# A new order for the first stage of an attention and two-FFN kernel on one core

## Chip, cores and metric

The kernel runs on one core of one Trainium2 chip. The metric is the device time of one execution in microseconds (us): the median of 3 runs before the change is 557.69 us (557.67 to 558.53).

## What is computed

A chunked attention with decays (a state-space form), then an FFN with a squared ReLU, then a bilinear FFN. Cut to what matters here:

```python
# x: 4 x 8 x 768 x 32, a: 4 x 8 x 768, B, C: 4 x 8 x 768 x 16; chunk by chunk along the 768
cum = np.cumsum(log(clip(a)), axis=-1)
L = np.exp(cum[:, :, :, None] - cum[:, :, None, :]) * causal
y_intra = einsum('bhij,bhjd->bhid', einsum('bhin,bhjn->bhij', C, B) * L, x)
y_inter = einsum('bhin,bhnd->bhid', C, state) * exp(cum)[..., None]
state = exp(sum(la))[..., None, None] * state + einsum('bhjn,bhjd->bhnd', B * decay_from_j, x)
# then, on 3072 tokens of 256:
x = relu(x @ w_in) ** 2 @ w_out          # 256 -> 2048 -> 256
x = ((x @ w1) * (x @ w2)) @ w3 @ w_out2  # 256 -> 1024 -> 1024 -> 256
```

## The kernel before

**Tiles.** The 3072 tokens are cut into six tiles of 512. For each tile the attention is worked out in chunks of 96 tokens; two chunks make a unit. The first stage, `startup`, does the six chunks (units 0, 1, 2) of tile 0, prepares units 3 and 4, and converts the first pieces of the weights. After it a loop goes through phases: A (the squared-ReLU FFN) and B (the bilinear FFN) of each tile, with the attention of the next tile placed between the matmuls. Weights arrive as 64-bit numbers, 512 KB a piece (`conv_load`), and are made into a high and a low float part by ScalarE (`conv_words`: L196, L198; `conv_parts`: L230), VectorE (`conv_bits`: L207, L210; `split_lo`, L141) and partly GpSimd (L228).

**The chain of the first stage.** `a` and `masks` are loaded; the logarithm (L343), then matmuls with the masks (L419, L455) give `e_first` (L422) and `dec` (L459). For a unit and each quarter q of its heads `unit_e1` (L663, L668 on TensorE, L671 on ScalarE) gives the decay factors e. `unit_pad` (L602) and `unit_bi` (L607) lay out C and B, `unit_g0` (L637) multiplies them into four PSUM banks, and `unit_m0` (L679, VectorE) multiplies a bank with its e. `chunk_pre` (L578, GpSimd) scales the chunk's x and B, `state` (L717 on TensorE, L724 on ScalarE) hands the state to the next chunk, and `value` (L755, then L144 and L141) gives the output of a chunk in `xt`. The first matmul of phase A (L819) needs all of `xt`.

**Order.** `startup` runs under `in_order()`, so each engine carries out its instructions in the order in which the function's calls stand. All loads go through SyncE's queue by `dma` (L93), in program order; a load also waits until the load eight places earlier has landed. B and C of the first batch come in two parts: the first 256 columns (`batch_load(s, 0, 1)`) and the rest (`batch_load(s, 1, 3)`); s is 0 for B, 1 for C. `unit_split` writes the split B and C of a later unit to DRAM (`hl_d`), and `unit_bc` loads them back in twelve small loads as `bt` and `cb`, for the matmuls of L618.

Of the kernel before, what the change touches and what calls it, by code (L numbers as in the profile page):

```python
# [7 lines left out]
F32 = mybir.dt.float32  # L8
# [7 lines left out]
P = 128  # L16
# [42 lines left out]
def kernel(  # L59
# [19 lines left out]
    nc = tc.nc  # L79
# [9 lines left out]
    ps_g = ctx.enter_context(tc.tile_pool(name="ps_g", bufs=2, space=PSUM))  # L89
    ps_y = ctx.enter_context(tc.tile_pool(name="ps_y", bufs=1, space=PSUM))  # L90

    def dma(out, in_):
        tc.keep_in_program_order(nc.sync.dma_start(out=out, in_=in_))  # L93

    keep = tc.keep_in_program_order

# [34 lines left out]
    def new_tmp():  # L131
        return tmp.tile([P, 512], F32, tag="tmp", name="tmp")
# [148 lines left out]
    pick = [gp.tile([P, H, P], F32R, tag="gp", name="pick") for k in range(2)]  # L281
    ident = wts.tile([P, P], F32R, tag="wa9", name="ident")
    nmask = act1.tile([P, P], F32R, tag="cmask", name="nmask")[:, :CH]
    m_rel = new_tmp()
    m_oth = new_tmp()
    la = new_tmp()[:, :256]
    lps = new_tmp()
    lp = lps[:, :192].rearrange("p (k c) -> p k c", k=3)
    lp4 = lps[:, 192:320].rearrange("p (v d c) -> p v d c", v=4, d=2)

    def constants():
        def diagonal(v, base=0, step=1, fill=1.0):
# [12 lines left out]
        raw = wts.tile([P, 512], F32, tag="wa10", name="raw")
        sel, one, low = raw[:, :64].rearrange("r (p c) -> r p c", p=4), raw[:, 64:192], raw[:, 192:192 + CH]
        nc.gpsimd.memset(cb.bitcast(F32), 0.0)
        nc.gpsimd.memset(raw[:, :192 + CH], 0.0)
        for base in (0, -16):
            diagonal(sel, base, 32, -1.0)  # L310
        diagonal(one.unsqueeze(1), 0, 0)
        causal(low.unsqueeze(1), NEVER)
        nc.gpsimd.memset(id2, 0.0)
        for p in range(4):
            diagonal(id2[32 * p:32 * p + 32].unsqueeze(1), 0, 0)
        nc.gpsimd.memset(idc, 0.0)
# [15 lines left out]
    def decays_load(k):
        if k == 0:
            dma(out=la, in_=a)
        elif k == 1:
            dma(out=m_rel, in_=masks[:, 0:512])
        else:
            c = (slice(256, 392), slice(0, 256))[k - 2]
            dma(out=m_oth[:, c], in_=masks[:, 512 + c.start:512 + c.stop])

    def decays_ln():
        nc.vector.tensor_scalar(out=la, in0=la, scalar1=1e-6, scalar2=1.0, op0=ALU.max, op1=ALU.min)
        nc.scalar.activation(  # L343
            lp.rearrange("p k (u h) -> p u k h", u=8), la[:, :192].rearrange("p (u k h) -> p u k h", u=8, k=3), AF.Ln
        )

        def put(copy, v, r, r_in, k):
            copy(lp4[r, v], lp[r_in, k, :2 * H].unsqueeze(1).to_broadcast([r.stop - r.start, 2, 2 * H]))

        put(nc.scalar.copy, 0, slice(0, P), slice(0, P), 0)  # L350
        put(nc.scalar.copy, 3, slice(0, P), slice(0, P), 2)
# [3 lines left out]
        warm = const.tile([P, 1], F32, name="warm")  # L355
        nc.scalar.activation(warm, la[:, :1], AF.Exp)

    def rel(b, i, n, nb=1):
# [120 lines left out]

    batch_0 = {}  # L480

    def batch_load(s, u0, u1):
        if s not in batch_0:
            batch_0[s] = wts.tile([P, S], F32, tag=f"wa{15 - s}", name="raw0")
        dma(
            out=batch_0[s].rearrange("p (u t) -> p u t", t=UT)[:, u0:u1],
            in_=raw_in[u0:u1].rearrange("u p (s t) -> s p u t", s=2)[s],
        )
# [117 lines left out]
    def unit_bi(c0, c1):  # L606
        nc.vector.tensor_copy(bi[:, c0:c1, :CH], batch_0[0][:, c0 * CH:c1 * CH].rearrange("p (c i) -> p c i", i=CH))  # L607
# [445 lines left out]
    def startup():  # L1053
        ys = {}

        def y0(g):
            ys[g] = new_mm()[:, :2 * CH].rearrange("p (h i) -> p h i", h=2)
            chunk_y_mm(g, ys[g])

        ds = [y_bank[:, 256 * (g % 2):256 * (g % 2) + 256] for g in range(FIRST[1])]  # L1060

        def state(g):
            chunk_ds(g, ds[g])
            if g + 1 < FIRST[1]:
# [10 lines left out]
        decays_load(0)  # L1075
        decays_load(1)
        decays_load(2)
        decays_load(3)
        batch_load(0, 0, 1)
        batch_load(1, 0, 1)  # L1080
        chunk_xb(0)
        chunk_xb(1)
        batch_load(0, 1, 3)
        batch_load(1, 1, 3)
        chunk_xb(2)
        chunk_xb(3, "w124")
        chunk_xb(4, "w125")
        chunk_xb(5, "w126")
        conv_load(1)
        unit_load(4)  # L1090
        conv_load(2)
        picks, rounded = constants()
        decays_ln()
        picks(0, nc.vector)
        rounded()
# [3 lines left out]
        decays_e_first()  # L1099
        picks(1, nc.gpsimd)  # L1100
        nc.vector.tensor_copy(bi[:, :, CH:], id2.unsqueeze(1).to_broadcast([P, FIRST[1], 32]))
        decays_cols()
        unit_bi(0, 2)
        unit_pad(0)
        chunk_pre(0)
        for q in range(4):
            unit_e1(0, q)
        unit_g0(0)
        unit_bi(2, 6)
        unit_pad(1)  # L1110
        chunk_pre(1)
        state(0)
        m0(0)
        chunk_pre(2)
        unit_e1(1, 0)
        unit_e1(1, 1)
        unit_split(3, "w120")
        state(1)
        unit_rows(bt)
        chunk_pre(3)  # L1120
        value(0)
        unit_e1(1, 2)
        unit_e1(1, 3)
        unit_pad(2)
        unit_g0(1)
        state(2)
        chunk_pre(4)
        m0(1)
        value(1)
        conv_load(2)  # L1130
        unit_bc(3)
        chunk_xb(6)
        unit_e1(2, 0)
        unit_e1(2, 1)
        conv_words(0)
        state(3)
        chunk_pre(5)
        value(2)
        unit_e1(2, 2)
        unit_e1(2, 3)  # L1140
        conv_bits(0)
        unit_g0(2)
        state(4)
        value(3)
        decays_e(0)
# [6 lines left out]
        value(4)
        chunk_xb(7)
        conv_words(1)
        value(5)
        state(5)
        conv_load(1)
        conv_bits(1)
        unit_split(4, "w121")
        chunk_xb(8)  # L1160
        conv_load(1)
# [150 lines left out]
```

## Time and profile before

| | |
|---|---|
| median of 3 runs | 557.69 us |
| profiled execution, its own time | 559.61 us |
| its span from first to last instruction | 557.9 us |
| mean granted TensorE clock | 0.993 |
| TensorE matmul, busy | 544.0 us (98%) |
| VectorE, busy | 367.6 us (66%) |
| ScalarE, busy | 284.3 us (51%) |
| GpSimd, busy | 88.1 us (16%) |

Engines are named PE (TensorE), DVE (VectorE), ACT (ScalarE), POOL (GpSimd) and SP (SyncE). PE is busy for 98% of the span; of its 13.9 us of idle time some 10 lie before 100 us. A busy PE is not PE at its peak: the ends of its matmuls are modelled, and the granted clock says at which of its two levels (1.2 and 2.4 GHz) it ran.

### The profile page before, as it was taken

What the parts mean: (1) busy time and instruction counts of PE and PEld (TensorE: products, weight loads), DVE (VectorE), ACT (ScalarE), POOL (GpSimd) and SP (SyncE); (2) the same over time, 40 slices, a digit from 0 to 9 for tenths busy, and PEclk for the clock granted to TensorE, in tenths of its full rate; (3) what the DMA queues carried; (4) which work ended last, traced back from release to release, by engine and by line L of the source; (5) the groups of instructions that cost most, each with busy time, mean ns of one, the idle gap of its engine ahead of it and who ended that gap; (6) DMA issues with size and microseconds to landing.
All of it is one profiled execution on the core that took longest, in us unless ns stands there. A gap on an engine that the chain in (4) does not pass through costs nothing.

```text
span 557.9 us, 9140 instructions
## 1 busy us (share of the span) xinstructions
PE 544.0 (98%) x3340; PEld 448.5 (80%) x3340; DVE 367.6 (66%) x665; ACT 284.3 (51%) x543; POOL 88.1 (16%) x136
## 2 busy tenths in 40 slices
PE   7979999999999999999999999999999999999997
PEld 5757777889888888888888888888888888888886
DVE  5689999987989575576576556574566474554431
ACT  6699768877875322354333354342435332444332
POOL 7344750000000221004031004020012010000000
PEclk9889999999999999999999999999999999999999
DMA  8697592143454561067250066120173220100001
GB/s 235 231 307 225 176 374 91 39 152 114 164 173 126 135 160 53 0 156 177 68 133 17 16 156 170 24 79 1 36 168 100 57 70 0 39 0 2 0 1 38
DMA packets 56573, 59.46 MB, mean 107 GB/s; under 512 B 33360, under 2 KB 44624, under 8 KB 56528
## 3 DMA queue, kind: packets, MB, share of 16 engines
q1 hardware_dynamic: 56528, 58.88, 36.8%
q8 instruction: 26, 0.43, 0.3%
q14 instruction: 19, 0.16, 0.1%
HBM read 50.20 MB, written 8.65 MB: 105 GB/s over the span
## 4 chain that ended last, share of the span: by engine, by line
PE 81%; DVE 8%; ACT 4%; DMA 4%; issue 1%; SPq 1%; DVEq 0%; ACTq 0%
PE mm L819 43%; PE acc L866 19%; PE acc L919 10%; PE mm L257 4%; PE acc L928 2%; PE y L755 2%; PE g L618 2%; DVE gp L141 2%; DMA xb<-in_xb_dram 1%; DMA raw<-in_raw_dram 1%; DVE cvs L207 1%; DVE wa L141 1%; SPq L93 1%; DVE cvs L210 1%; DMA u<-in_w_dram 1%
## 5 line engine op out<-in xcount | busy, mean ns | idle before, releaser
L819 PE MATMUL mm<-xt,wa 128*128 128x512 f32 x576 | 148.7, 395 | 3.2 <-DVE wa L141 2.0
L849 ACT CAST gp<-tmp 128x512 fp32r<-128x512 f32 x144 | 89.3, 622 | 119.4 <-DVE tmp L907 64.3
L866 PE MATMUL acc<-gp,wa 128*128 128x512 f32 x576 | 146.4, 392 | 1.3 <-DVE gp L141 0.7
L141 DVE TENSOR_TENSOR gp<-tmp,gp 128x512 fp32r<-128x512 f32 x144 | 103.0, 718 | 62.7 <-ACT gp L849 61.9
L819 PE MATMUL mm<-x,w 128*128 128x512 f32 x576 | 143.4, 392 | 0.0
L819 PEld LDWEIGHTS mm<-xt,wa 128*128 128x128 f32 x576 | 107.4, 190 | 26.8 <-ACT tmp L833 2.4
L866 PEld LDWEIGHTS acc<-gp,wa 128*128 128x128 f32 x576 | 106.4, 188 | 24.5 <-DVE gp L141 1.5
L819 PEld LDWEIGHTS mm<-x,w 128*128 128x128 f32 x576 | 105.9, 188 | 21.7 <-ACT tmp L899 0.2
L833 ACT ACTIVATE tmp<-mm 128x512 f32<-128x512 f32 x96 | 57.3, 597 | 50.9 <-PE mm L819 50.2
L919 PE MATMUL acc<-gp,w3o 128*128 128x512 f32 x240 | 63.7, 391 | 0.0
L843 DVE TENSOR_TENSOR tmp<-tmp 128x512 f32<-128x512 f32 x68 | 46.9, 692 | 24.0 <-ACT tmp L833 23.5
L559 POOL TENSOR_SCALAR_AFFINE_SELECT e<-e 96x768 f32<-96x768 f32 x26 | 25.3, 985 | 236.3 <-DMA e<-e_d 228.9
L907 DVE TENSOR_TENSOR tmp<-tmp,mm 128x512 f32<-128x512 f32 x48 | 33.0, 687 | 42.9 <-PE mm L819 42.4
L919 PEld LDWEIGHTS acc<-gp,w3o 128*128 128x128 f32 x240 | 44.8, 188 | 9.4
L899 ACT COPY tmp<-mm 128x512 f32<-128x512 f32 x48 | 28.2, 587 | 41.0 <-PE mm L819 40.7
L578 POOL TENSOR_TENSOR xb<-xb,dec 96x256 f32<-96x256 f32 x32 | 23.1, 723 | 91.9 <-DMA xb<-in_xb_dram 89.2
L624 DVE TENSOR_TENSOR e<-g,e 128x384 f32<-128x384 f32 x52 | 27.6, 551 | 6.5 <-PE g L618 6.0
L257 PE MATMUL mm<-wo,w 128*128 128x256 f32 x128 | 23.7, 284 | 0.4 <-DVE w L141 0.3
L745 DVE SCALAR_TENSOR_TENSOR xb<-xb,through,y 32x64 f32<-32x64 f32 x72 | 20.3, 282 | 3.1 <-PE y L717 1.3
L257 PEld LDWEIGHTS mm<-wo,w 128*128 128x128 f32 x128 | 20.6, 190 | 2.0 <-DVE w L141 1.0
L618 PEld LDWEIGHTS g<-cb,bt 96*128 96x128 f32 x96 | 16.6, 190 | 3.3
L257 PE MATMUL mm<-wo2l,w 128*128 128x256 f32 x64 | 18.1, 283 | 0.0
(111 smaller groups left out, 476.9 us busy)
## 6 DMA issues: line engine op xcount, KB each, us to landing
u<-in_w_dram SPq DMA_DIRECT2D x24, 512.0 KB, 3.9
ua<-in_w_dram SPq DMA_DIRECT2D x16, 512.0 KB, 7.0
e<-e_d SPq DMA_DIRECT2D x40, 192.0 KB, 5.1
xb<-in_xb_dram SPq DMA_DIRECT2D x32, 192.0 KB, 3.8
bt<-hl_d SPq DMA_DIRECT2D x78, 48.0 KB, 2.1
hl_d<-gp SPq DMA_DIRECT2D x9, 384.0 KB, 2.6
cb<-hl_d SPq DMA_DIRECT2D x66, 48.0 KB, 2.0
out_dram<-gp SPq DMA_DIRECT2D x20, 128.0 KB, 3.0
```

Source lines behind the costliest of these rows:

```text
L141: return nc.vector.tensor_tensor(out=lo, in0=src, in1=hi.bitcast(F32), op=ALU.subtract)
L257: nc.tensor.matmul(acc[:, :DM], v[:, l, e % 4 * P:(e % 4 + 1) * P], wo2[1 + e // 2][r][:, e % 2 * DM:(e % 2 + 1) * DM], start=(n == 0), st ...
L618: nc.tensor.matmul(ps[:, 2 * pp:2 * pp + 2], w, un["c2"][:, pr, :, j * CH:(j + 1) * CH], start=True, stop=True)
L624: nc.vector.tensor_tensor(out=m, in0=ps, in1=m, op=ALU.mult)
L819: i = nc.tensor.matmul(ps, w[m][:, l, col + k * P:col + (k + 1) * P], rhs[k][:, r, :], start=((l, r, k) == (1, 0, 0)), stop=((l, r, k) == ...
L833: nc.scalar.activation(r, ps, AF.Relu)
L843: nc.vector.tensor_tensor(out=g32, in0=r, in1=r, op=ALU.mult)
L849: nc.scalar.copy(g[:, 0, :], d[k])
L866: i = nc.tensor.matmul(acc["x2", t][e], wa[m][:, l, 256 + e * P:256 + (e + 1) * P], g[:, r, :], start=(m == 0 and n == 0), stop=(m == MF - ...
L899: nc.scalar.copy(s, ps)
L907: nc.vector.tensor_tensor(out=p32, in0=prods[t, m], in1=ps, op=ALU.mult)
L919: nc.tensor.matmul(acc["o"][e].rearrange("p s e -> p (s e)"), w3o[m // 2][:, l, m % 2, e * P:(e + 1) * P], g[:, r, :], start=(m == 0 and n ...
```

## The change

Four things. The order of the calls in `startup` is another one. The products of `unit_m0` and the factors of `unit_e1` are called one quarter at a time and interleaved, where all four of a unit stood together. `masks` comes in one transfer of 904 columns into one tile, where it came in three into two tiles. The first parts of B and C are issued from ScalarE's queue, behind a small Ln that has its table loaded ahead of them. Besides, GpSimd's clearing of `cb` moves behind the making of the constants.

```diff
-    def dma(out, in_):
-        tc.keep_in_program_order(nc.sync.dma_start(out=out, in_=in_))
+    def dma(out, in_, eng=nc.sync):
+        tc.keep_in_program_order(eng.dma_start(out=out, in_=in_))
...
-    m_rel = new_tmp()
-    m_oth = new_tmp()
+    m_all = wts.tile([P, 904], F32, tag="wo0", name="masks")
+    m_rel, m_oth = m_all[:, :512], m_all[:, 512:]
...
         nc.vector.memset(lp4, 0.0)
+        nc.vector.memset(warm, 1.0)
+        nc.scalar.activation(warm, warm, AF.Ln)
...
-        nc.gpsimd.memset(cb.bitcast(F32), 0.0)
         nc.gpsimd.memset(raw[:, :192 + CH], 0.0)
...
         nc.gpsimd.memset(bt[64:96, :, :, CH:].bitcast(F32), 0.0)
+        nc.gpsimd.memset(cb.bitcast(F32), 0.0)
...
-    def batch_load(s, u0, u1):
+    def batch_load(s, u0, u1, eng=nc.sync):
...
+        picks, rounded = constants()
+        decays_load()
         chunk_xb(0)
         chunk_xb(1)
+        batch_load(0, 0, 1, nc.scalar)
+        picks(0, nc.vector)
+        batch_load(1, 0, 1, nc.scalar)
+        conv_load(1)
+        batch_load(1, 1, 3)
         batch_load(0, 1, 3)
...
+        unit_e1(0, 0)
...
+        unit_e1(1, 3)
         chunk_pre(0)
-        for q in range(4):
-            unit_e1(0, q)
+        unit_e1(0, 1)
+        unit_e1(1, 2)
         unit_g0(0)
+        unit_m0(0, 0)
+        unit_m0(0, 1)
+        unit_e1(0, 2)
+        unit_e1(0, 3)
...
+        unit_pad(1)
+        unit_bi(2, 6)
+        state(1)
+        unit_g0(1)
```

**VectorE, from the layout of unit 0's B and C on.** `bi` and `cp` are the laid-out B and C, raw_111 and raw_113 (now raw_153 and raw_156) the loaded ones, e the products, `hl` the split for unit 3. Before:

```order
L607 COPY bi<-raw_111 128x2x96
L602 TENSOR_SCALAR cp<-raw_113,halves 128x192 x2
L607 COPY bi<-raw_111 128x4x96
L602 TENSOR_SCALAR cp<-raw_113,halves 128x192 x2
L679 TENSOR_TENSOR e<-g,e 128x2x192 x4
L141 TENSOR_TENSOR hl<-raw_111,hl 128x192
L141 TENSOR_TENSOR hl<-raw_113,hl 128x192
L141 TENSOR_TENSOR xt<-mm,xt 128x2x96
L602 TENSOR_SCALAR cp<-raw_113,halves 128x192 x2
L679 TENSOR_TENSOR e<-g,e 128x2x192 x4
```

With the change:

```order
L605 COPY bi<-raw_153 128x2x96
L600 TENSOR_SCALAR cp<-raw_156,halves 128x192 x2
L677 TENSOR_TENSOR e<-g,e 128x2x192 x4
L600 TENSOR_SCALAR cp<-raw_156,halves 128x192 x2
L605 COPY bi<-raw_153 128x4x96
L677 TENSOR_TENSOR e<-g,e 128x2x192 x2
L141 TENSOR_TENSOR xt<-mm,xt 128x2x96
L677 TENSOR_TENSOR e<-g,e 128x2x192 x2
L600 TENSOR_SCALAR cp<-raw_156,halves 128x192 x2
```

The four products of unit 0 now stand ahead of the two instructions that need the rest of B and C, and the split for unit 3 is gone from here: it stands behind the last product of unit 2.

**SyncE's queue, its first loads.** ua is a piece of weights, xb a chunk of x and B. Before:

```order
L93 DMA tmp<-in_a_dram 128x256
L93 DMA tmp<-in_masks_dram 128x512
L93 DMA tmp<-in_masks_dram 128x136
L93 DMA tmp<-in_masks_dram 128x256
L93 DMA raw_111<-in_raw_dram 128x256
L93 DMA raw_113<-in_raw_dram 128x256
L93 DMA xb<-in_xb_dram 96x512 x2
L93 DMA raw_111<-in_raw_dram 128x2x256
L93 DMA raw_113<-in_raw_dram 128x2x256
L93 DMA xb<-in_xb_dram 96x512 x4
L93 DMA ua_129<-in_w_dram 128x1024
```

With the change:

```order
L93 DMA tmp<-in_a_dram 128x256
L93 DMA masks<-in_masks_dram 128x904
L93 DMA xb<-in_xb_dram 96x512 x2
L93 DMA ua_158<-in_w_dram 128x1024
L93 DMA raw_156<-in_raw_dram 128x2x256
L93 DMA raw_153<-in_raw_dram 128x2x256
L93 DMA xb<-in_xb_dram 96x512 x2
L93 DMA ua_178<-in_w_dram 128x1024
L93 DMA ua_180<-in_w_dram 128x1024
L93 DMA xb<-in_xb_dram 96x512 x2
```

A piece of weights now goes ahead of the rest of C and of B, and two more ahead of the last two chunks.

**SyncE's queue, around the loads for unit 3.** Before:

```order
L93 DMA hl_d_326<-hl 128x2x384
L93 DMA ua_399<-in_w_dram 128x1024
L93 DMA ua_401<-in_w_dram 128x1024
L93 DMA bt<-hl_d_326 32x4x96 x6
L93 DMA cb<-hl_d_326 16x4x192 x6
```

With the change:

```order
L93 DMA hl_d_485<-hl 128x2x384
L93 DMA xb<-in_xb_dram 96x512
L93 DMA ua_518<-in_w_dram 128x1024
L93 DMA xb<-in_xb_dram 96x512
L93 DMA hl_d_558<-hl 128x2x384
L93 DMA bt<-hl_d_485 32x4x96 x6
L93 DMA cb<-hl_d_485 16x4x192 x6
L93 DMA ua_572<-in_w_dram 128x1024
```

The twelve loads for unit 3 now stand behind the write of unit 4's split (hl_d_558), and the seventh piece of weights, ua_572, behind them.

## Rows read from the trace of the kernel before

**Rows 1.** Windows: length, then PE, PEld, DVE, ACT, POOL busy us, PE's clock, DMA share, GB/s

```profile
10.00:20.00 10.00, 8.43 (x100) 6.86 (x101) 6.61 (x16) 5.35 (x15) 5.89 (x13) 0.83 1.03 355
20.00:30.00 10.00, 8.80 (x152) 7.43 (x150) 6.76 (x15) 8.03 (x21) 0.80 (x2) 1.00 0.54 153
...
40.00:50.00 10.00, 9.19 (x36) 6.96 (x35) 9.96 (x15) 9.42 (x21) 7.24 (x9) 0.92 0.63 192
...
200.00:300.00 100.00, 100.00 (x621) 82.52 (x620) 63.41 (x118) 37.87 (x68) 18.20 (x27) 1.00 0.41 103
```

**Rows 2.** Waits of VectorE from 0 to 30 us: total us, times, longest

```profile
DVE xt L141 <- ACT xt L144: 3.3, 3, 2.1
DVE e L679 <- PE g L637: 1.9, 1, 1.9
DVE tmp L342 <- DMA tmp<-in_a_dram: 1.8, 1, 1.8
DVE cp L602 <- DMA raw<-in_raw_dram: 1.7, 1, 1.7
```

**Rows 3.** Timeline of VectorE: start us, us, what; in brackets the idle time before it

```profile
4.50 0.69 DVE L321 CAST pick<-raw 128x1024 fp32r<-128x1024 f32 x1
...
6.49 1.06 DVE L1101 COPY bi<-id 128x192 f32<-128x192 f32 x1
...
11.29 0.55 DVE L602 TENSOR_SCALAR cp<-raw,halves 128x192 f32<-128x192 f32 x2 [1.71 <-DMA raw<-in_raw_dram]
11.75 1.95 DVE L679 TENSOR_TENSOR e<-g,e 128x384 f32<-128x384 f32 x4
...
28.89 0.69 DVE L210 SCALAR_TENSOR_TENSOR cvs<-ua,cvs 128x512 uint32<-128x512 uint32 x1
```

**Rows 4.** Timeline of ScalarE

```profile
3.31 0.36 ACT L343 ACTIVATE tmp<-tmp 128x192 f32<-128x192 f32 x1 [1.22 <-DVE tmp L342]
...
7.13 1.71 ACT L671 ACTIVATE e<-mm 128x384 f32<-128x384 f32 x4
...
39.63 0.68 ACT L196 ACTIVATE cvs<-ua 128x512 f32<-128x512 f32 x1
```

**Rows 5.** Timeline of TensorE

```profile
8.79 0.93 PE L637 MATMUL g<-cp,bi 32*128 32x192 f32 x16 [0.47 <-DVE cp L602]
...
15.95 1.66 PE L637 MATMUL g<-cp,bi 32*128 32x192 f32 x16
...
35.04 0.59 PE L618 MATMUL g<-cb,bt 96*128 96x192 f32 x4
...
37.85 4.61 PE L819 MATMUL mm<-xt,wa 128*128 128x512 f32 x12
```

**Rows 6.** DMA issues of short stretches: KB each, us from issue to landing

```profile
tmp<-in_masks_dram SPq DMA_DIRECT2D x1, 256.0 KB, 2.8
...
raw<-in_raw_dram SPq DMA_DIRECT2D x2, 128.0 KB, 3.0
...
raw<-in_raw_dram SPq DMA_DIRECT2D x1, 256.0 KB, 6.2
...
ua<-in_w_dram SPq DMA_DIRECT2D x1, 512.0 KB, 8.2
...
u<-in_w_dram SPq DMA_DIRECT2D x1, 512.0 KB, 3.1
```

**Rows 7.** Timeline of SyncE's queue: start us, us of issuing

```profile
1.25 1.37 SPq L93 DMA_DIRECT2D tmp<-in_masks_dram  x3
...
7.45 0.54 SPq L93 DMA_DIRECT2D ua<-in_w_dram  x1
...
19.74 3.70 SPq L93 DMA_DIRECT2D bt<-hl_d  x6
23.54 2.73 SPq L93 DMA_DIRECT2D cb<-hl_d  x6
```

**Rows 8.** Windows, a stretch of the first stage with another granted clock

```profile
14.20:17.60 3.40, 3.40 (x27) 2.78 (x24) 1.48 (x4) 1.30 (x3) 1.86 (x4) 0.50 1.03 397
```

More of the change, by code (lines that the diff above doesn't have):

```diff
@@ L289 @@
     lp4 = lps[:, 192:320].rearrange("p (v d c) -> p v d c", v=4, d=2)
+    warm = const.tile([P, 1], F32, name="warm")
     def constants():
@@ L330, in constants, with decays_load @@
         return picks, rounded
[L332 to L339, printed above, removed]
+    def decays_load():
+        dma(out=la, in_=a)
+        dma(out=m_all, in_=masks)
     def decays_ln():
@@ L354, in decays_ln @@
             put(nc.vector.tensor_copy, v + 1, slice(r, r + n), slice(r_in, r_in + n), k)
-        warm = const.tile([P, 1], F32, name="warm")
         nc.scalar.activation(warm, la[:, :1], AF.Exp)
@@ L486, in batch_load @@
             out=batch_0[s].rearrange("p (u t) -> p u t", t=UT)[:, u0:u1],
-            in_=raw_in[u0:u1].rearrange("u p (s t) -> s p u t", s=2)[s],
+            in_=raw_in[u0:u1].rearrange("u p (s t) -> s p u t", s=2)[s], eng=eng,
         )
@@ L1073, in m0 @@
                 unit_m0(u, q)
[L1075 to L1080, printed above, removed]
+        picks, rounded = constants()
+        decays_load()
         chunk_xb(0)
         chunk_xb(1)
+        batch_load(0, 0, 1, nc.scalar)
[3 more added lines that the diff above has]
+        batch_load(1, 1, 3)
         batch_load(0, 1, 3)
-        batch_load(1, 1, 3)
+        rounded()
+        decays_ln()
         chunk_xb(2)
[L1086 to L1095, printed above, removed]
         nc.vector.tensor_reduce(
@@ L1098, in startup @@
         )
-        decays_e_first()
+        chunk_xb(3, "w124")
+        conv_load(2)
         picks(1, nc.gpsimd)
         nc.vector.tensor_copy(bi[:, :, CH:], id2.unsqueeze(1).to_broadcast([P, FIRST[1], 32]))
+        decays_e_first()
         decays_cols()
+        unit_e1(0, 0)
+        chunk_xb(4, "w125")
         unit_bi(0, 2)
         unit_pad(0)
+        unit_e1(1, 3)
         chunk_pre(0)
-        for q in range(4):
-            unit_e1(0, q)
+        unit_e1(0, 1)
+        unit_e1(1, 2)
@@ L1108, in startup @@
         unit_g0(0)
-        unit_bi(2, 6)
-        unit_pad(1)
+        unit_m0(0, 0)
+        unit_m0(0, 1)
+        unit_e1(0, 2)
+        unit_e1(0, 3)
+        unit_rows(bt)
+        state(0)
         chunk_pre(1)
-        state(0)
-        m0(0)
+        unit_m0(0, 2)
+        conv_words(0)
+        unit_m0(0, 3)
         chunk_pre(2)
+        unit_e1(2, 3)
         unit_e1(1, 0)
         unit_e1(1, 1)
-        unit_split(3, "w120")
-        state(1)
-        unit_rows(bt)
-        chunk_pre(3)
@@ L1121, in startup @@
[L1121 to L1130, printed above, removed]
-        unit_bc(3)
[L1132 to L1145, printed above, removed]
@@ L1146, in startup @@
-        m0(2)
+        chunk_xb(5, "w126")
+        unit_pad(1)
+        unit_bi(2, 6)
+        state(1)
+        unit_g0(1)
+        unit_m0(1, 0)
+        unit_m0(1, 1)
+        chunk_pre(3)
+        value(1)
+        unit_e1(2, 2)
+        unit_e1(2, 0)
+        state(2)
+        unit_e1(2, 1)
+        conv_words(1)
+        unit_m0(1, 3)
+        unit_m0(1, 2)
+        unit_load(4)
+        state(3)
+        unit_pad(2)
+        unit_g0(2)
+        unit_m0(2, 1)
+        value(0)
+        value(2)
@@ new lines, in startup @@
+        unit_load(5)
+        chunk_pre(4)
+        unit_m0(2, 2)
+        unit_m0(2, 0)
+        conv_load(2)
+        state(4)
+        chunk_xb(6)
+        unit_m0(2, 3)
+        chunk_pre(5)
+        decays_e(0)
+        conv_bits(0)
+        unit_split(3, "w120")
+        value(4)
+        conv_parts(0)
+        state(5)
+        value(3)
+        chunk_xb(7)
+        conv_load(1)
+        chunk_xb(8)
+        decays_e(1)
+        conv_bits(1)
+        conv_words(2)
+        value(5)
+        unit_split(4, "w121")
@@ L1147, in startup @@
+        unit_bc(3)
         conv_load(1)
-        unit_load(5)
-        conv_parts(0)
-        decays_e(1)
+        conv_load(1)
         decays_e_out()
[L1152 to L1161, printed above, removed]
+        conv_parts(1)
         owed[6] = lambda: chunk_hand(5, ds[5])
-        conv_words(2)
-        conv_parts(1)
         at_piece[0] = 2
```

## Prediction

> **What bounds the kernel now.** I read the windows of the whole program first. From 200 us on PE is busy all the time, 100 of 100 us at full clock [rows 1]: nothing there can be gained by another order of the first stage. From 40 to 50 us DVE is busy 9.96 of 10 us and PE 9.19; but from 10 to 30 us PE has 17.2 of 20 and DVE 13.4 [rows 1]. So the first 30 us wait for something, what follows is work without gaps, and whatever the first stage gives up or wins should arrive at the end one for one, as long as the stretch behind it does not start to wait.
>
> Next the waits of DVE, the engine that is full afterwards, in those 30 us [rows 2]: 3.3 us for ScalarE's halves of `xt`, 1.9 us for PE's g, 1.8 us for `a`, 1.7 us for the rest of C. The timeline shows the last one's price: C's rest lands at 11.3 (6.2 us behind its issue [rows 6]), DVE lays out `cp` of unit 1, and only then multiplies unit 0's four products, from 11.75 to 13.70 [rows 3], although unit 0 needs nothing of that load and PE had its g ready at 8.79 + 0.93 = 9.72 [rows 5]. Everything later in the stage hangs on these products.
>
> **The change, part by part.** All times are in the span of the profiled execution, 557.9 us, whose own time of 559.61 stands 1.9 above the median of 557.69. I work out by how much the end moves and take that from the median.
>
> *Up to unit 0's g.* Ln starts at 3.31 after `a`, with ScalarE idle for 1.22 us [rows 4]; its table load is in that kernel ahead of the wait, too. The two DMA issues that ScalarE gets fit into this gap at SyncE's price (1.37 us for three, 0.46 each [rows 7]: 0.9). Cost nothing; if one issue cost twice as much on ScalarE, Ln would come 0.6 late. One transfer for `masks` saves two issues on SyncE. It carries 452 KB; a lone 512 KB took 3.1 us [rows 6], so it lands at 1.25 + 3.1 = 4.4, about when its first matmul can start, some 0.7 us behind Ln's end. Bound above: before, 384 KB (`a` and the first 256 KB of masks) had landed at 1.25 + 2.8 = 4.05 [rows 6, 7], and the other 196 KB at the slowest rate below, 187 KB a us, take 1.0: 5.1, so 0 to 0.7 late, and I take 0. The casts of `pick`, `ident` and `nmask` (0.69 for the first [rows 3], 1.1 together) move ahead of `a`, into DVE's wait of 1.8: that wait shrinks by 1.1. GpSimd's clearing of `cb` moves behind the constants and only makes room for these casts; its next work begins as before. The copy of `id` into `bi`, 1.06 us at 6.49 [rows 3], moves ahead of `e_first`, so `cp` of unit 0 is ready a microsecond earlier, and the 0.47 us that PE waited for it [rows 5] go: g from 8.3 to 9.25.
>
> *Unit 0.* Four e take 1.71 us on ScalarE, 0.43 each [rows 4]. Now six stand in line, two for unit 1; the last two wait for g on PE and are done near 10.5. Four products of 0.49 (1.95 [rows 3]) from 9.3 on, the last held back by its e: done at 11.2, where it was 13.70. The wait for C's rest, 1.7, is off this path.
>
> *Unit 1 and the reordered loads.* A piece of weights (512 KB) goes ahead of the rests of C and B. Before, the first piece landed at 7.45 + 8.2 = 15.65 [rows 6, 7] and with it 3012 KB: from 4.05 on 2628 KB in 11.6 us, 227 KB a us. By 11.3, when C's rest lands [rows 3], it was 1732 KB: 1348 KB in 7.2 us, 187 KB a us. Now 2244 KB stand up to the rest of B, 580 of them in by 4.4; the other 1664 need 7.3 us at the first rate and 8.9 at the second, so it lands at 11.7 to 13.3. I take 12.0, nearer the first, since the load includes a piece of weights as that stretch does. Unit 1's `cp` is made by then (11.2 + 0.55); `bi` follows, and g takes 0.93: done near 13.4, where it was 15.95 + 1.66 = 17.6 [rows 5]. The chunks x4 and x5 come behind two more pieces, about 17 to 20; their first use is about there, and only DVE's later work would notice.
>
> *The first parts of B and C.* No row shows two queues at work. In SyncE's queue these loads took 3.0 us [rows 6]; issued at 2.3 and 2.7 that gives 5.3 and 5.7, and they are needed at 6.5. Bound above: they stand behind x0, x1 and the piece of weights, 896 KB at 227, and land at 9.5; then all of unit 0 moves by 2.4, of which unit 1's wait for B's rest absorbs a part, and 1.8 us of the gain go. I take the row, cost 0.
>
> The Trainium skill (DMA: Bandwidth & Descriptors, section on queues, rings and completion order) says that each DMA engine takes turns between the queues that it has work for; by that the two loads get their share at once and the sum stands, while one common line would leave 1.8 us less. No run here shows which.
>
> *Sum over DVE's waits up to one point,* the second piece's last bit operation, done at 28.89 + 0.69 = 29.6 [rows 3]; the same instructions stand ahead of it in both orders but for a split of 0.6 us, which the new order does just behind it, with ScalarE ready. Wait for `a`: -1.1. For C's rest: -1.7. For g: before 1.9; now three, for unit 0 from 7.8 to 9.3 (1.5), unit 1 from 12.4 to 13.4 (1.0) and unit 2 about as much (1.0), with 0.1 for an e: +1.7. For `xt`: before 3.3, of which 2.1 in one piece because ScalarE had two conversions ahead of it; the new order does these while ScalarE would wait for g, and I leave 0.8: -2.5. Together **-3.6**: done at 26.0.
>
> *Carrying it on.* SyncE's queue must keep up. The split for unit 4 ends at 26.6; behind its write stand the twelve loads of unit 3, 3.70 + 2.73 = 6.4 us of issuing [rows 7], then the seventh piece of weights: issued at 33.0, landed 3.1 later [rows 6], at 36.1. ScalarE took the seventh piece at 39.63 [rows 4]; moved by 3.6, it asks for it at 36.0. So it is just in time, and beyond that loads are early. DVE is full from there [rows 1], and the 3.6 us reach the end. **557.7 - 3.6 = 554.1.**
>
> **Rivals.**
> *A. Unit 3's loads hold PE.* PE takes its instructions in order, and L618 needs all twelve loads, which moved from 19.7 to about 26.6 and land by 35. Before, L618 ran at 35.04 and the next L819 at 37.85 [rows 5]. Ready at 35 now, the next L819 can start at 35.6: 2.3 gained there, not 3.6, and a second delay of the seventh piece by 0.5 would agree with it. 557.7 - 2.3 = 555.4. For it: twelve issues in a row are in the trace; against: before, PE waited there for e anyway.
> *B. The gain is hidden.* What follows is paced by the arrival of the weights: same bytes, same queue, the seventh piece two microseconds later than I say. Then ScalarE's conversions, and DVE behind them, go on at 38 or later, within 1 us of before: 557.0. Against it: DVE, not DMA, is full at 40 to 50 us (DMA share 0.63 [rows 1]).
> *C. The clock: slower.* Between 14.2 and 17.6 us PE ran at 0.50 [rows 8], its lower level of 1.2 GHz, after it had waited for the products; g took 1.66 there and 0.93 at full clock [rows 5]. From 10 to 30 us PE's work is 17.2 us with that stretch, 15.5 at full clock, some 13.3 of it in this stage. The new order leaves PE 16.7 us for it (9.25 to 26.0), 3.4 to spare. Each stretch of that length at the lower level costs 1.7: two are free, and 3.4 + 3.6 = 7.0 are used up by four. With the whole stage at the lower level PE ends 13.3 later than its work needs, 6.3 more than slack and gain: 564. For it: PE's work comes in smaller portions with waits between them; against: in 30 us of such portions the trace shows one stretch.
> The Trainium skill (TensorE: Matmul & The Clock Gate, Part 1) says that the throttled state is the default and activity lifts it; with PE waiting more often the rule speaks for C, and the row of 0.50 behind a wait agrees.
> *D. More than I say.* B's rest lands by 11, the stretch at the lower clock falls out (1.7 on PE), x2 to x5 are in time: 5.3 gained, 552.4.
>
> **How the numbers follow.** A run of this kernel can be told from no change at 0.2%, 1.1 us. The forecast has 0.48 (553.2 to 555.0, by its terms of 0 to 0.9), A 0.23, B 0.13, C 0.08, D 0.08. Faster: forecast, A, D and a little of B, 0.80; same: the rest of B, 0.11; slower: C and what is unknown, 0.09. The range goes from D to B's middle, 552.3 to 557.1; outside are C and half of B.
>
> **What would show it.** Right: unit 0's products end near 11.2 and unit 1's g near 13.4 on the timelines; DVE's wait for C's rest is gone from its waits; the second piece's bit operations end near 26; the seventh piece is taken near 36; behind 50 us everything stands 3.6 earlier. Wrong: B's and C's first parts land after 6.5, `masks` after 4.5, a granted clock of 0.5 in several stretches before 26 us, or PE idle for microseconds ahead of L616 (L618 before).

## The result, and the profile after

The changed kernel takes **564.07 us**, median of 10 runs (560.74 to 566.81), the kernel before 558.39 (557.67 to 558.98) beside it: a ratio of 1.0100, 95% interval 1.0076 to 1.0125. It is slower by 1%; forecast was 554.1, faster. The profiled execution of after took 566.81, the longest of the ten, with a span of 565.1, 7.2 above that of before. A second trace (the run r2 below) has a span of 560.6, so the waits read here may be larger than those of a middling execution.

The windows of after, columns as in [rows 1]: from 200 us on TensorE is busy all the time, as before; between 70 and 90 us something has changed.

```profile
10.00:20.00 10.00, 9.84 (x136) 8.08 (x138) 6.25 (x15) 8.62 (x21) 7.37 (x17) 1.00 1.05 309
20.00:30.00 10.00, 7.84 (x145) 6.62 (x135) 8.94 (x20) 7.39 (x20) 0.60 (x2) 1.00 0.46 149
...
70.00:80.00 10.00, 5.31 (x26) 3.71 (x24) 4.47 (x10) 6.73 (x12) 2.51 (x4) 0.85 1.02 348
80.00:90.00 10.00, 10.00 (x56) 7.78 (x55) 9.30 (x17) 4.96 (x10) 4.22 (x6) 0.81 0.96 382
...
200.00:300.00 100.00, 100.00 (x646) 82.18 (x645) 62.89 (x122) 37.75 (x70) 16.69 (x25) 1.00 0.41 105
```

The half clock of [rows 8] is gone from 10 to 20 us. From 70 to 80 PE is busy 5.31 of 10 us and DVE, the engine that was to be full, 4.47; the mean clock is 0.85 there and 0.81 in the ten behind. Over the whole execution it is 0.994, in before 0.993, so the clock by itself does not explain the 7.2 us.

**The first stage.** VectorE's timeline of after, from 11 to 28 us, answers [rows 3]:

```profile
11.31 2.07 DVE L677 TENSOR_TENSOR e<-g,e 128x384 f32<-128x384 f32 x4 [2.07 <-PE g L635]
...
24.02 0.61 DVE L141 TENSOR_TENSOR hl<-raw,hl 128x192 fp32r<-128x192 f32 x2
...
26.43 0.69 DVE L210 SCALAR_TENSOR_TENSOR cvs<-ua,cvs 128x512 uint32<-128x512 uint32 x1
```

Unit 0's products end at 11.31 + 2.07 = 13.4, where 11.2 was forecast and 13.70 was before. The second piece's bit operations end at 27.1 (forecast 26.0, before 29.6). The waits of VectorE from 0 to 30 us answer [rows 2]. Those for `a` and for C's rest are gone, and of that for `xt` 0.2 is left; the forecast had left 0.7 for `a` and 0.8 for `xt`. But one for `masks` is new, and three for g take 4.4 (forecast 3.6 with an e).

```profile
DVE e L677 <- PE g L635: 4.4, 3, 2.1
DVE halves L1086 <- DMA masks<-in_masks_dram: 1.8, 1, 1.8
...
DVE xt L141 <- ACT xt L144: 0.2, 1, 0.2
```

TensorE's timeline says the same in its own rows (compare [rows 5]); the wait in its last row but one is the long one:

```profile
6.56 0.87 PE L417 MATMUL mm<-masks,tmp 128*32 128x96 f32 x32 [1.65 <-DMA masks<-in_masks_dram]
...
14.63 0.93 PE L635 MATMUL g<-cp,bi 32*128 32x192 f32 x16
...
36.66 0.66 PE L616 MATMUL g<-cb,bt 96*128 96x192 f32 x4 [0.45 <-DMA cb<-hl_d]
...
79.07 2.93 PE L817 MATMUL mm<-xt,wa 128*128 128x512 f32 x6 [4.47 <-DVE wa L141]
81.80 2.52 PE L864 MATMUL acc<-gp,wa 128*128 128x512 f32 x6
```

**The place of the loss.** VectorE at that point in after, then in before:

```profile
72.11 1.02 DVE L622 TENSOR_TENSOR e<-g,e 128x384 f32<-128x384 f32 x2
77.39 0.43 DVE L206 TENSOR_SCALAR uo<-uo 128x512 uint32<-128x512 uint32 x1 [4.26 <-DMA uo<-in_w_dram]
77.73 0.68 DVE L210 SCALAR_TENSOR_TENSOR cvs<-ua,cvs 128x512 uint32<-128x512 uint32 x1
78.33 0.68 DVE L141 TENSOR_TENSOR wa<-cvs,wa 128x512 fp32r<-128x512 f32 x1
```

```profile
70.72 1.01 DVE L624 TENSOR_TENSOR e<-g,e 128x384 f32<-128x384 f32 x2
...
72.74 0.93 DVE L141 TENSOR_TENSOR wa<-cvs,wa 128x512 fp32r<-128x512 f32 x1
...
74.80 1.09 DVE L141 TENSOR_TENSOR wa<-cvs,wa 128x512 fp32r<-128x512 f32 x1
75.81 0.84 DVE L206 TENSOR_SCALAR uo<-uo 128x512 uint32<-128x512 uint32 x1
```

TensorE in before, at the products that follow:

```profile
73.77 1.66 PE L819 MATMUL mm<-xt,wa 128*128 128x512 f32 x6
```

`uo` is the first piece of another weight (`w_out` of the last FFN), needed far later; L206 shifts its low words. In before it stands behind two low parts of `wa`; in after it stands ahead of both. Its load has not landed there, and VectorE, which takes its work in order, stands for 4.26 us with the `wa` that TensorE waits for behind the shift. TensorE waits 4.47 and then takes 2.93 us for six products at a lowered clock, where six took 1.66 in before. **The change's diff doesn't touch this place**: instructions behind the startup are put in order by a planner that estimates times (`schedule_with_timeline_sim`), and with another startup it chose another order.

The load of `uo` is late, too. SyncE's queue, after then before:

```profile
24.66 0.38 SPq L93 DMA_DIRECT2D hl_d<-hl  x1
...
29.10 3.06 SPq L93 DMA_DIRECT2D bt<-hl_d  x6
32.20 2.77 SPq L93 DMA_DIRECT2D cb<-hl_d  x6
35.02 0.91 SPq L93 DMA_DIRECT2D ua<-in_w_dram  x2
...
69.39 1.09 SPq L93 DMA_DIRECT2D uo<-in_w_dram  x2
```

```profile
66.81 0.91 SPq L93 DMA_DIRECT2D uo<-in_w_dram  x2
```

The queue stood idle for 7.2 us ahead of the write at 24.66 (one wait, put down to VectorE), then issued unit 3's twelve loads from 29.1 to 35.0 (before 19.7 to 26.3 [rows 7]) and the seventh piece of weights at 35.02. Three theories were possible: **O**, the planner's order behind the startup; **Q**, SyncE's queue, made late by the late split of unit 3; **S**, the late start through the masks. The expectations add **K**, the half clock itself.

### The profile page after: what moved, and what is told of

The parts are those of the page before. It is cut to its first block, busy times and chain, and to the rows that moved or that the text cites. A ratio compares the mean times of both kernels' runs of the same rounds, so it can differ in the third digit from the quotient of the medians.

```text
span 565.1 us, 9141 instructions
## 1 busy us (share of the span) xinstructions
PE 544.2 (96%) x3340; PEld 447.5 (79%) x3340; DVE 365.1 (65%) x666; ACT 284.4 (50%) x544; POOL 85.3 (15%) x136
## 4 chain that ended last, share of the span: by engine, by line
PE 83%; DMA 8%; DVE 4%; ACT 2%; SPq 2%; issue 1%; DVEq 0%; ACTq 0%
PE mm L817 43%; PE acc L864 19%; PE acc L917 10%; PE mm L257 3%; SPq L93 2%; PE acc L926 2%; PE y L753 2%; PE g L616 2%; DMA u<-in_w_dram 1%; DMA hl_d<-gp 1%; DMA uo<-in_w_dram 1%; DMA e_d<-tmp 1%; DMA masks<-in_masks_dram 1%; DVE gp L141 1%; PE y L715 1%
## 5 line engine op out<-in xcount | busy, mean ns | idle before, releaser
L817 PE MATMUL mm<-xt,wa 128*128 128x512 f32 x576 | 148.6, 395 | 7.5 <-DVE wa L141 5.2
L864 PE MATMUL acc<-gp,wa 128*128 128x512 f32 x576 | 148.1, 394 | 2.5 <-ACT gp L847 2.0
L817 PE MATMUL mm<-x,w 128*128 128x512 f32 x576 | 143.4, 392 | 0.0
L817 PEld LDWEIGHTS mm<-xt,wa 128*128 128x128 f32 x576 | 107.0, 189 | 31.5 <-DVE wa L141 5.5
L817 PEld LDWEIGHTS mm<-x,w 128*128 128x128 f32 x576 | 105.9, 188 | 21.7 <-ACT tmp L897 0.2
L897 ACT COPY tmp<-mm 128x512 f32<-128x512 f32 x48 | 28.2, 587 | 41.9 <-PE mm L817 41.6
```

The costliest lines, as they stand in the source:

```text
L817: i = nc.tensor.matmul(ps, w[m][:, l, col + k * P:col + (k + 1) * P], rhs[k][:, r, :], start=((l, r, k) == (1, 0, 0)), stop=((l, r, k) == ...
L864: i = nc.tensor.matmul(acc["x2", t][e], wa[m][:, l, 256 + e * P:256 + (e + 1) * P], g[:, r, :], start=(m == 0 and n == 0), stop=(m == MF - ...
L897: nc.scalar.copy(s, ps)
```

## The experiments

All ratios are against the kernel before, run beside, with the 95% interval. 0.001 is 0.56 us.

| run | what | ratio | interval |
|---|---|---|---|
| after | the change | 1.0100 | 1.0076 to 1.0125 |
| e1 | after, split of unit 3 early | 1.0099 | 1.0068 to 1.0131 |
| e2 | before, split of unit 3 late | 1.0027 | 1.0008 to 1.0045 |
| e3 | after, first B and C from SyncE | 1.0078 | 1.0056 to 1.0100 |
| e4 | before, products ahead of unit 1's layout | 0.9976 | 0.9955 to 0.9997 |
| e5 | after, shifts of uo held | 1.0065 | 1.0040 to 1.0090 |
| e6 | after, shifts held behind all wa | 1.0037 | 1.0024 to 1.0050 |
| e7 | e6 with e3 | 1.0020 | 0.9996 to 1.0044 |
| e8 | before, two shifts early | 0.9987 | 0.9966 to 1.0009 |
| e9 | e7, split early | 1.0011 | 0.9991 to 1.0030 |
| e10 | before, first B and C from ScalarE | 0.9979 | 0.9961 to 0.9998 |
| e11 | e6, masks in three transfers | 1.0034 | 1.0015 to 1.0054 |
| e12 | e4 with e10 | 0.9997 | 0.9985 to 1.0009 |
| e13 | e9, masks in three transfers | 1.0025 | 1.0010 to 1.0041 |
| e14 | startup of after, order of before behind | 1.0030 | 1.0017 to 1.0044 |
| e15 | startup of before, order of after behind | 1.0028 | 1.0019 to 1.0037 |
| e16 | e13's startup, order of before behind | 1.0015 | 1.0004 to 1.0026 |

### Is it the late split, or the start? (e1, e2, e3)

e1 moves two calls of after, e2 the same two of before the other way:

```diff
         unit_g0(1)
+        unit_split(3, "w120")
...
         chunk_xb(6)
+        unit_bc(3)
...
         conv_bits(0)
-        unit_split(3, "w120")
...
         unit_split(4, "w121")
-        unit_bc(3)
```

> The changed kernel, with the split of unit 3 (and its write hl_d) put back to right behind unit 1's g, and its twelve loads bt and cb behind the load of xb 6, so that SyncE's queue no longer stands idle for 7.2 us until 24.66. Theory Q (the order left SyncE's queue idle and pushed twelve small loads, the two e_d writes and the seventh piece of weights into a stretch in which the queue has no room): the write goes out near 16 to 17, bt and cb between 20 and 27, the seventh piece lands before 37, PE's wait of 4.5 us for wa near 75 us is gone, 554 to 558 us. Theory S (the loss comes from the start, where the masks landed at 6.42 instead of 4.3): nothing of the start changes, so 561 to 566 us, as the changed kernel. Theory K (the loss is the half clock behind 77 us and has nothing to do with these loads): 561 to 566 us with windows of granted clock under 0.9 behind 70 us.

> The kernel before, with only the split of unit 3 (and its write) moved behind the parts of the first piece, and its twelve loads behind the split of unit 4, where the change has them. The start, the products and all other loads stay. Theory Q: the queue stands idle before the late write, the twelve loads go out behind 30 us, the seventh piece lands behind 39, and the kernel is slower, 560 to 565 us. Theory S or K: within 0.2% of before, 557.5 to 559.5 us, since nothing of the start moves and nothing on the way needs unit 3 before 35 us.

e1 gained nothing. The write went out at 18.72, not 16 to 17, with the queue held behind it, and `uo` was issued at 68.57, 0.8 earlier than in after. VectorE still had the new order, but waited only 0.8 us for `uo`. So in this trace part of the loss lies elsewhere, and before that place: ScalarE stands 3.34 us until a write from the tile `gp` to `hl_d` has ended, and TensorE 2.44 behind it.

```profile
60.05 0.62 ACT L847 CAST gp<-tmp 128x512 fp32r<-128x512 f32 x1 [3.34 <-DMA hl_d<-gp]
```

The wait for `uo` is thus one way in which the time is lost, not the only one. e2 shows what the late split costs by itself: 1.5 us (0.4 to 2.5), less than Q expected and more than S or K. TensorE stands there for `cb`, which is part of unit 3's loads; it had no such wait in before [rows 5]:

```profile
37.18 1.14 PE L618 MATMUL g<-cb,bt 96*128 96x192 f32 x4 [1.96 <-DMA cb<-hl_d]
```

Q is a part, a small one.

e3:

```diff
         decays_load()
+        batch_load(0, 0, 1)
+        picks(0, nc.vector)
+        batch_load(1, 0, 1)
         chunk_xb(0)
         chunk_xb(1)
-        batch_load(0, 0, 1, nc.scalar)
-        picks(0, nc.vector)
-        batch_load(1, 0, 1, nc.scalar)
         conv_load(1)
```

> The changed kernel, with the first parts of B and C issued from SyncE's queue again, ahead of x0 and x1; the masks stay one transfer. Theory S (ScalarE's queue delayed the masks): masks land at 4.3 to 4.6, the first parts of B and C near 5.7 and 6.1, the whole first stage stands 2 us earlier, and the time falls to 554 to 558. Theory Q: the same early start, but the queue still waits for the split of unit 3, so at most the 2 us come through: 561 to 564 us.

```profile
25.48 0.69 DVE L210 SCALAR_TENSOR_TENSOR cvs<-ua,cvs 128x512 uint32<-128x512 uint32 x1
```

The masks' transfer took 3.6 us instead of 5.2 and the second piece's bit operations ended at 25.48 + 0.69 = 26.2: **the first stage that the forecast described, at the forecast's time**. The kernel still took 563.07. VectorE waited 3.8 us for `uo`, PE 3.8 for `wa`, the clock was 0.75 from 70 to 80. S falls as the main cause, and with it the sentence that what the first stage wins reaches the end.

### The part that was to bring the gain, alone (e4)

```diff
-        unit_bi(2, 6)
-        unit_pad(1)
         chunk_pre(1)
         state(0)
         m0(0)
+        unit_bi(2, 6)
+        unit_pad(1)
```

> The kernel before, with the layout of bi and cp of unit 1 (the DVE work that waits for the rest of B and C) moved behind unit 0's four products and nothing else. This is the part of the change that the forecast took for its main gain. If what the first stage wins reaches the end: the wait of 1.7 us for C's rest goes, products of unit 0 done near 12, split of unit 3 and its loads a microsecond earlier, 556.5 to 557.5 us. If what follows is paced by the arrival of weights and not by the first stage: 558.0 to 559.0, the same as before.

1.3 us (0.2 to 2.5), within what was expected. The forecast had priced this wait at 1.7. The planner's order behind this startup is that of before, and no wait for `uo` appears.

### Holding the shifts of uo (e5, e6, e7, e8)

In `conv_bits`, behind the shift (e6 and e7; e5 names the pieces that they followed before):

```diff
+            if MF <= i < MF + 10:
+                tc.add_manual_dep(
+                    nc.cur_bb.bb.instructions[-1], low_done[MF - 1],
...
+                )
```

> The changed kernel, whose shifts of the low words of the w_out pieces (L206, tile uo) are held behind the low parts (wa) of the pieces that they followed in the kernel before: the first two behind the fourteenth piece, the next two behind the fifteenth, the rest behind the sixteenth. Startup, loads and queues stay. Theory O (the planner behind the startup moved two of these shifts ahead of wa on VectorE, the first stands for 4.26 us until its load lands at 77.36, and PE, which needs the wa behind it, waits 4.5 us and then runs at half clock): the wait of PE for wa near 75 us is gone or below 1 us, the granted clock is 1.00 from 70 to 90, and the lead of 0.5 to 1.5 us that the changed kernel had at 70 us comes through: 556 to 559 us. Theory Q (SyncE's queue is late anyway, so what PE loses at 75 it loses a piece later): 561 to 566.

> The changed kernel, with all shifts of low words of the w_out pieces and the first w3 pieces (L206) held behind the low part of the sixteenth, last wa. Theory O: as with the pieces held behind the fourteenth to sixteenth or better, since no wa can stand behind a late load of uo: 556 to 559 us; VectorE has room for the shifts between 90 and 120 us. Theory Q: 561 to 566 us.

> The changed kernel with the first parts of B and C issued from SyncE's queue (as in the run with that part alone, which stood 2.5 to 3.7 us ahead of before until 70 us and lost it between 70 and 80) and all shifts of uo held behind the last wa. Theory O: the lead of the first stage comes through whole: 554 to 556 us, faster than before by 2.5 to 4. Theory Q: 561 to 565.

> The kernel before, with the shifts of the first two uo pieces put ahead of the wa of the thirteenth and fourteenth piece, where the changed kernel has them. Their loads land at 73.2 and 75.0 there, and these wa were made at 72.74 and 74.80, so VectorE stands for about 1 us in place of 4.3. Theory O (order and lateness together set the price): 558.5 to 560 us. Theory Q or S: 558.0 to 558.7, as before.

Holding these instructions gives back 0.0035 (e5) and 0.0063 (e6), 2.0 and 3.5 of 5.6 us, and the waits of VectorE in e6 and e7 have none for `uo` between 66 and 84 us. Both fall short of the 556 to 559 expected, and e5 lies in the range given for Q: in its trace VectorE still waits 1.4 us for `uo`, and in e6 ScalarE still waits 6.6 us in all for `ua` between 48 and 84 us, up to 2.5 at a time. The clock is not what is left (theory K): the profiled execution of e5 has a mean clock of 1.00 and still a span of 559.1, and the ratio of e5 is 1.0065. e7 stands 0.0017 below e6; the intervals overlap. e8 puts two shifts early in the kernel before. It cost nothing, where O had expected a wait of about 1 us: the first `uo` was issued at 66.0 there and landed 6.8 us later, when the shift's turn came, and VectorE never waited for it. In these traces the early place is dear only where the load is late.

### Second looks (r1, r2)

> The kernel before once more, for a second trace. In a run whose startup is that of before, the second piece's last bit operation ended at 27.3 us and PE kept full clock up to 35 us, where the profiled execution of before had 29.6 and a stretch at 0.50 from 14.2 to 17.6. If that stretch was an accident of one execution, this trace has none before 20 us and the operation ends at 27.0 to 27.8; if it belongs to the kernel, 29 to 30.

> The changed kernel once more, for a second trace. Theory O: VectorE again waits for the load of uo ahead of wa, by 2 to 5 us, and PE behind it, with a half clock stretch near 80; the masks land at 5.7 to 6.5 and the second piece's last bit operation ends at 26.5 to 27.5, no more than 1 us ahead of a trace of before without the half clock.

r1 is the kernel before, unchanged. Its windows, then its VectorE:

```profile
14.20:17.60 3.40, 3.40 (x56) 2.86 (x51) 2.94 (x8) 1.89 (x5) 2.57 (x6) 1.00 1.03 388
...
40.00:50.00 10.00, 7.92 (x26) 5.44 (x25) 9.96 (x16) 7.91 (x18) 6.27 (x8) 0.83 0.65 190
```

```profile
27.46 0.69 DVE L210 SCALAR_TENSOR_TENSOR cvs<-ua,cvs 128x512 uint32<-128x512 uint32 x1
```

No half clock at 14.2, and the second piece is done at 28.2, not 29.6; in e8, with before's startup, at 26.57 + 0.69 = 27.3. The stretch of [rows 8] belonged to one execution. r1 is 1.4 us ahead at 28 us, and yet its span is 557.8, against 557.9. The lead was lost on the way: the `wa` that before makes at 72.74 is made at 72.08 in r1. The stretch at a lower clock between 40 and 50 us does not show where it went, since before has one there too (0.92 [rows 1]). r2, the changed kernel again, waits less for `uo` than the 2 to 5 expected, and its time is 562.39 against 566.81:

```profile
DVE uo L206 <- DMA uo<-in_w_dram: 1.6, 2, 1.3
```

Its second piece is done at 27.81 + 0.69 = 28.5, a microsecond behind the expected stretch and behind r1: no lead at all.

### Which part of the start is dear (e9, e10, e11, e12, e13)

> The run with loads from SyncE's queue and all shifts of uo behind the last wa (558.99 us), with the split of unit 3 also put back, this time with ScalarE's two copies right behind the value of state 0, ahead of three e and of the first piece's conversion, so that the write goes out near 15 us, and the twelve loads behind xb 6. If the late split costs what it cost in the kernel before (1.4 us): 557.0 to 558.0. If the queue is no bound once uo is out of the way: 558.7 to 559.3.

> The kernel before, with only the first parts of B and C issued from ScalarE's queue. If the two queues share the bandwidth, all three parts of the masks land later (0.5 to 1.5 us) and the first stage with them: 558.5 to 560. If ScalarE's queue is free, as the forecast took it: 557.5 to 558.5.

> The changed kernel with all shifts of uo held behind the last wa (560.13 us), and the masks again in three transfers on tiles of their own; the first parts of B and C stay on ScalarE's queue. If one large transfer is what made the masks late beside ScalarE's loads: the first 256 KB land by 5.0 (6.4 before), the first stage moves up by 1 to 1.5, 558.5 to 559.3 us. If the two queues share out the time in any case: 559.8 to 560.5.

> The kernel before with the two parts that each gained alone: unit 0's products ahead of the layout of unit 1 (557.37, 0.9976), and the first parts of B and C from ScalarE's queue (557.56, 0.9979). If the two gains add: 556.4 to 556.9 us. If both remove the same wait, that for the rest of C: 557.2 to 557.7.

> The changed order of the first stage with all that the other runs found dear undone: shifts of uo behind the last wa, first parts of B and C from SyncE's queue, masks in three transfers, the split of unit 3 and its loads early. What is left is the order of the products, e and weights. If that order is worth the 2 to 3 us that the forecast gave it: 555.0 to 556.5 us. If its gain was read from one execution with a half clock stretch that most do not have: 557.5 to 559.0, no different from before.

e9 puts the split of unit 3 behind `unit_bi(2, 6)`, on top of e7. Unit 1's layout and ScalarE's copies then stand ahead of three e and of the first piece's conversion. No difference from e7 can be told. e10 gives `nc.scalar` to the two `batch_load(.., 0, 1)` of before and nothing else. e11 and e13 load `masks` as before, `[0:512]`, `[768:904]`, `[512:768]`, on tiles of their own.

ScalarE's two loads are the same in e10 and after; their place is not. ScalarE's timeline of after, then of e10:

```profile
0.81 1.28 ACT L308 ACT_TABLE_LOAD   x1 [0.81 <-PEq L1304]
1.28 0.87 ACTq L93 DMA_DIRECT2D raw<-in_raw_dram  x2
...
39.42 0.68 ACT L196 ACTIVATE cvs<-ua 128x512 f32<-128x512 f32 x1 [1.43 <-DMA ua<-in_w_dram]
```

```profile
0.81 0.89 ACTq L93 DMA_DIRECT2D raw<-in_raw_dram  x2
1.73 1.28 ACT L343 ACT_TABLE_LOAD   x1 [1.73 <-PEq L1298]
```

The landings, KB each and us from issue: after, then e11, then e10.

```profile
masks<-in_masks_dram SPq DMA_DIRECT2D x1, 452.0 KB, 5.2
...
raw<-in_raw_dram ACTq DMA_DIRECT2D x2, 128.0 KB, 4.8
```

```profile
tmp<-in_masks_dram SPq DMA_DIRECT2D x1, 256.0 KB, 4.2
raw<-in_raw_dram ACTq DMA_DIRECT2D x2, 128.0 KB, 4.1
```

```profile
raw<-in_raw_dram ACTq DMA_DIRECT2D x2, 128.0 KB, 3.2
tmp<-in_masks_dram SPq DMA_DIRECT2D x1, 256.0 KB, 3.3
```

Beside loads from ScalarE the masks' first 256 KB take 4.2 or 3.3 us, alone 2.8 [rows 6]. Three transfers in place of one (e11 against e6) change nothing that can be told, so the masks' lateness comes from the second queue, as e3 showed by taking its loads away. e10 and e11 issue the masks alike. That they land 0.9 later in e11 may come from the start of ScalarE's loads, 1.28 there, beside the masks, and 0.81 in e10; no run moves that start alone. e10 gains 1.2 us (0.1 to 2.2), although its masks landed later. e12 adds e4 to it and is at 0.9997: the two gains don't add, and e12, which holds both, shows neither. e13 undoes everything that was found dear and is at 1.0025. It misses the 555 to 556.5 and the 557.5 to 559 expected, and it isn't below e9, from which it differs by the masks alone. Differences of this size, a microsecond, can't be put down to a part.

### Startup and order exchanged (e14, e15, e16)

Behind the startup the program issues the same instructions in both kernels, so the order of one can be laid on the other: a chain of dependences that carry no wait, over the instructions of all four engines that stand elsewhere (`behind` lists their numbers).

```diff
     out_last(NTILE - 1)
...
+    for run in behind:
+        for prev, i in zip(run, run[1:]):
+            tc.add_manual_dep(
+                made_as[f"I-{i}"], f"I-{prev}",
...
+            )
```

> The changed kernel with its startup as it is, and behind the startup every instruction of VectorE, ScalarE, TensorE and GpSimd held in the order in which the planner had put them in the kernel before (the two orders differ in 78 places of VectorE's first 100 there, 67 of ScalarE's first 113, 191 of TensorE's first 291, 11 of GpSimd's first 34, and nowhere behind). Theory O: the loss lies in that order and not in the startup; no shift of uo waits ahead of wa, no conversion waits for its weights ahead of the copies that TensorE needs: 557.5 to 559.5 us. Theory Q or S (late loads and late masks of the startup cost the time in any order): 561 to 565 us.

> The reverse: the kernel before with its own startup, and behind it every instruction of the four engines in the order that the planner chose for the changed kernel. Theory O with the order alone: 560 to 564 us. Order and lateness together: the loads of uo land near 73 here, so the waits are about 1 us and not 4: 558.3 to 560. Theory Q or S: 557.8 to 558.8, as before.

> The new order of the first stage with masks in three transfers, first parts of B and C from SyncE's queue and the split of unit 3 early, and behind the startup the order of before on all four engines. This is the first stage of the forecast without any of the parts found dear. If that stage is worth what the forecast gave it: 555 to 556.5 us. If its gain was that of one slow trace: 557.5 to 558.7, as before.

VectorE in e14, where the order of before is back, then in e15:

```profile
72.00 0.93 DVE L141 TENSOR_TENSOR wa<-cvs,wa 128x512 fp32r<-128x512 f32 x1
...
74.05 1.09 DVE L141 TENSOR_TENSOR wa<-cvs,wa 128x512 fp32r<-128x512 f32 x1
75.07 0.42 DVE L206 TENSOR_SCALAR uo<-uo 128x512 uint32<-128x512 uint32 x1
```

```profile
69.96 1.01 DVE L624 TENSOR_TENSOR e<-g,e 128x384 f32<-128x384 f32 x2
71.30 0.92 DVE L206 TENSOR_SCALAR uo<-uo 128x512 uint32<-128x512 uint32 x1 [0.33 <-DMA uo<-in_w_dram]
72.14 0.68 DVE L210 SCALAR_TENSOR_TENSOR cvs<-ua,cvs 128x512 uint32<-128x512 uint32 x1
72.74 0.68 DVE L141 TENSOR_TENSOR wa<-cvs,wa 128x512 fp32r<-128x512 f32 x1
```

The new startup alone costs 0.0030 (1.7 us), the new order alone 0.0028 (1.6), both together 0.0100 (5.6): 2.3 us more than the sum (the 5.6 are known to 1.4). The rows fit: the same shift ahead of the same `wa` waits 0.33 us behind the old startup, and behind the new one 4.26 in the first trace and 1.6, over two waits, in r2. With the old order back, e14 shows no wait for `uo` at all.

What e14 has instead is rival A's wait, in TensorE's row for unit 3's loads:

```profile
36.41 1.14 PE L616 MATMUL g<-cb,bt 96*128 96x192 f32 x4 [3.62 <-DMA cb<-hl_d]
```

Its second piece is done at 25.73 + 0.69 = 26.4, ahead of both traces of before. But the products behind `cb` (L817) start at 38.20, behind the 37.85 of before [rows 5]: in this trace the lead of the new startup ends at unit 3's loads.

e16 is the new first stage with e9's early split, without ScalarE's loads and the one transfer, and with the old order behind. It is at 1.0015, 0.8 us slower (0.2 to 1.5), and has no wait for `cb`: **the first stage's order by itself is worth nothing**. Its second piece is done at 26.51 + 0.69 = 27.2, where r1 had 28.2 and e8 27.3.

## Why the prediction was wrong

*The step that failed* is the carrying on: "DVE is full from there [rows 1], and the 3.6 us reach the end". What the runs show in its place: the planner's new order and the late startup cost 1.6 and 1.7 us alone and 5.6 together, through waits behind that point. I looked at the order of the startup alone; the list of VectorE's instructions behind it had the shift of `uo` ahead of two `wa`, and the row of before that shows how little room there was: `wa` at 74.80, the shift at 75.81, right behind each other. What the forecast called "full" is a stretch of VectorE in which a wait of 4.3 us for one load holds up everything. Nor was what follows 30 us "work without gaps" in before; a window that [rows 1] leaves out has TensorE at 6.84 and VectorE at 8.69 of 10 us:

```profile
30.00:40.00 10.00, 6.84 (x28) 4.96 (x27) 8.69 (x14) 9.94 (x21) 4.62 (x7) 0.91 1.04 330
```

e3 reached 26.2 at the point where 26.0 was forecast and ended at 563; e14 has the same startup as after and ends 3.9 us (0.0070) below it.

*The point from which the gain was counted* was unlucky. The second piece's 29.6 contained a stretch at 0.50 that other traces of the same startup lack (28.2 and 27.3). Rival C named this stretch and priced it for the change; it was not taken out of before. Of the 3.6 us, 1.4 to 2.3 were in that one trace of before. Even a lead that exists, r1's 1.4 us, did not reach the end.

*"I take 0" for the masks*, with 0.7 as the bound: TensorE waits 1.65 for them. A lone transfer was taken as the row, and two loads of another queue ran beside this one. Without them the masks took 3.6 us, landing 0.5 later than the 4.4 forecast.

*"I take the row, cost 0" for B's and C's first parts:* 4.8 us to landing in the median instead of 3.0, and the price was paid by the masks. The Trainium skill (DMA: Bandwidth & Descriptors, section on queues, rings and completion order) says that each DMA engine takes turns between the queues that it has work for. The rows agree, since both queues' loads take longer side by side, but the forecast drew only the half of it that was good for these two loads.

*Unit 0 and unit 1*: products done at 13.4 (11.2), unit 1's g at 14.63 + 0.93 = 15.56 (13.4), both late by the masks' 1.65 and half a microsecond more. The mechanism, products ahead of unit 1's layout, was right: e4 gained 1.3 by it alone, though e12 did not repeat that gain.

*SyncE's queue*: the seventh piece was issued at 35.02 (33.0), took 4.3 us to land (3.1), and ScalarE took it at 39.42 after a wait of 1.43, where "just in time" at 36.0 stood; before took it at 39.63 [rows 4]. Rival B, "same bytes, same queue, the seventh piece two microseconds later than I say", described this (33.0 against 35.02), and had 0.13. It ended at "no change", though; that the same lateness meets an order that punishes it was no rival. Rival A's wait for unit 3's loads was 0.45 us in after, but 3.62 in e14, where the old order stands behind: its mechanism is real, and in after the new order puts other products ahead of that row. Rival C's half clock came at 70 to 90 us, behind the wait for `wa`, and not in the first stage.

*What stays open:* the 1.7 us of the new startup with the old order were not split further. The wait for `cb` in e14 and e2 points to the late split, for which e2 gives 1.5 us. But e16, where split and loads are undone, still leaves 0.8, and with the new order e1 and e9 gained nothing by an early split. The differences between e9, e11 and e13 are about a microsecond. How the 5.6 us divide among the waits differs from trace to trace (4.26 us for `uo` in after, 1.6 in r2, 0.8 in e1).

## What to carry to other kernels

Where a planner lays the rest of the program by estimated times, an edit of one stage edits everything behind it: compare the order of every engine over the whole program, look for instructions that wait for a load and now stand ahead of work that the critical engine needs, and ask when that load lands. Count a gain in a stage from more than one execution, and take a stretch at a lower clock out of the base first. To tell a stage's worth from the order behind it, hold the old order and change the stage alone.

## What the runs showed of the hardware

ScalarE's two DMA issues went out from 1.28 to 2.15, while its table load ran from 0.81 to 2.09: they don't wait for it to end. What they cost shows in the other queue's landing: 5.2 us for 452 KB beside them, 3.6 without (e3). The half clock comes and goes between executions of one program: one trace of before has it at 14.2 to 17.6 us and, by the mean of 0.92, again between 40 and 50; the next has none at 14.2 and 0.83 between 40 and 50, with spans of 557.9 and 557.8.
